# The turned g of the state tokens through V's two PSUM banks, and new places for the steps of the first two batches

## The chip, the cores and the metric

The kernel runs on one core of a Trainium2 chip. That core has five engines with an instruction queue each: TensorE (PE in the rows; PEld is its weight load), VectorE (DVE), ScalarE (ACT), GpSimd (POOL) and SyncE (SP), which issues nearly all the DMAs here. The metric is the device time of one execution in microseconds (us), lower being better. Three runs of the kernel before gave 486.24, 484.85 and 485.97 us, a median of 485.97 us.

## The reference, cut to what matters

Eight batches of 8 heads, 512 tokens and 32 state tokens go through attention in both directions. The result is 4608 rows of 512: eight times 512 tokens (the first part) and 32 state tokens. These rows go through a feed-forward layer with a piecewise activation, and then through a soft mixture of experts.

```python
def _attn_ref(x, state):                       # B, H, S, D = 8, 8, 512, 64; 32 state tokens
    a = softmax(x @ state^T / 8);   xread = a @ state
    a2 = softmax(state @ x^T / 8);  sread = a2 @ x
    return concatenate([xread, sread], axis=2)

def _moe_ref(x, w_in, w_out):                  # 4608 x 512, 512 x 2048, 2048 x 512
    h = x @ w_in
    g = np.where(h >= 1, h, np.where(h <= -1, 0.0, (h + 1) ** 2 / 4))
    return g @ w_out

def _moe2_ref(x, phi, w1, w2):                 # 8 experts of 4 slots
    logits = x @ phi
    slot_input = softmax(logits, axis=0)^T @ x
    slot_out[e] = relu(slot_input[e] @ w1[e]) @ w2[e]
    return softmax(logits, axis=1) @ slot_out
```

`w_in` and `w_out` come as 64-bit floats, and the kernel makes 32-bit floats of them on the chip.

## The kernel before

**Tiling.** The main loop goes over nine blocks `b`: the eight batches with 512 tokens each, and block 8 with the 256 state tokens of all batches. In each block `m` runs over 16 slices of 128 of the 2048 hidden columns. `attention(b)` makes the softmax of a batch, transposed; `vchunk(b, c)` multiplies the batch's state by a quarter `c` of `w_in`, so that `hstep(b, m)` gets a slice of h as V times the softmax, without the attention's output ever being made. In batch 0 h is two plain 32-bit products (line 529). From batch 1 on V and the softmax are each split into a high and a low half, and h is six products of halves (line 538): the high half is a ScalarE copy, the low half is V minus the high half, either by VectorE straight from PSUM (line 487) or by a second ScalarE copy `Vs` and a GpSimd subtraction (line 485). Lists in the table `CFG` (`lP0`, `lP1`, `lP`) name the pairs (c, G) that take the second way; G is one of the two PSUM banks of V. `Vs` shares its one buffer (`rot_q`) with `wsb` and `dR`.

**After h.** ScalarE makes c = relu(h/2 + 1/2); c is squared by GpSimd (letter E in `gv0`, `gv1`, line 568) or by ScalarE (letter S); VectorE makes g = min(max(h, 1), c) (line 592). The pool `psH` has three PSUM banks for h, so the fourth h after one waits until that one's g is made. VectorE turns g in blocks of 32x32 for later (`tstep`, line 612), `estep` multiplies a quarter of the g's by wp = w_out times phi, and `smblock` takes the running softmax over the tokens and accumulates g with its weights (`fall`, tiles FV and FX).

**The weights.** `conv_win(i)` for i = 0 to 7 and `conv_wo(i)` for i = 8 to 15 each turn a 1 MB stage of 64-bit words into 32-bit floats, by `words(i)`. For i in `dv` that is three VectorE instructions of 1024 columns (lines 154, 156, 158). For the others it is two byte moves into a rim (`LT`, `ast` or another tile), both by ScalarE or, for i in `pr`, the second by GpSimd (line 166), and two VectorE instructions (lines 170, 172). Two `conv_wo` make one of four `wps` products, whose ScalarE copy `wsb` is turned (line 197) and becomes a quarter of wp.

**Block 8.** The g of the state tokens are turned whole by TensorE: `tquarter(k)` (lines 601 to 609) turns four slices of 2x128 tokens, eight transposes of 128x128, into the tile gtp and copies them to `natS`. The tiles gtp come from `psH`, beside block 8's own h. `natS` is read by the products P in `smstate`, after which its buffers take weights of the experts. The experts' weights w1 and w2 (32 MB) are loaded by SP into whatever buffers come free, through the last third of the program.

**What sets the order.** For batches 2 to 7 TensorE's order is the order in which `steady` is written; everything else (batches 0 and 1, block 8, and the other engines throughout) is ordered by a scheduler when the program is built, from priorities in the order of the code. Lists of `CFG` say at which `m` a step is written: `cpos` the conversions, `at0` and `attA` the steps of attention 1 and 2, `V0` and `Vn` the V chunks, `E0` and `T0` the E quarters and the turned g's of batch 0, `a0n` how many steps of attention 0 come ahead of the first conversion. `warm` matmuls of 128x128 without use are issued behind the first scores.

Lines 116 and 122 are the helper `group` of matmuls side by side, line 127 the helper `act` of every ScalarE instruction.

Of the kernel before, what the change touches and what calls it, by code (L numbers as in the profile page):

```python
# [13 lines left out]
PSUM = bass.MemoryType.PSUM  # L14


CFG = {'no': 1, 'nl': 0, 'n0': (1, 12), 'nw': 512, 'nj': 'CABD', 'cw': (2, 2, 2, 4, 5, 6, 6, 7, 8, 8, 9, 11, 12, 13, 14, 15), 'pr': (0, 4), 'a0n': 6, 'w1p': (), 'r0': 0, 'sw': 1, 'whole': (4, 5, 6, 7), 'em': 8, 'lE': (0, 5, 8, 11), 'sV': (0, 4, 9, 12), 'sE': (7, 11, 15), 'sS': (1, 3, 5, 7), 'sN': 13, 'sM': (14, 14), 'gv7': 'EESESSSEESSSEEEE', 'cpos': (0, 1, 1, 3, 4, 4, 5, 7, 8, 10, 10, 12, 12, 15), 'at0': (5, 5, 5, 9, 9, 12, 13, 14, 14, 14), 'lP0': ((0, 0), (0, 1), (1, 0), (1, 1), (3, 0), (3, 1)), 'lP1': ((0, 1), (1, 0), (2, 0)), 'gv1': 'EEEEEEEEEESEEESE', 'f32': (0, 1, 2, 3), 'wsm': 14, 'xsP': 1, 'eng': ('PE',), 'wt8': (7, 8, 9, 10, 11, 12, 13, 14), 'wte': 'DA', 'wb': 12, 'gv6': (3, 5, 15), 'lP': ((0, 0), (0, 1), (1, 0), (2, 0), (3, 1)), 'attA': (3, 7, 9, 10, 11, 11, 11, 12), 'attB': (1, 11, 11, 12, 13), 'attN': (14, 15), 'dv': (3, 7, 8, 11), 'fl': -0.484375, 'hp': 2000, 'att7': (3, 5, 6, 7, 8, 10), 'og': 1, 'n3': 1, 'n3m': 10, 'wS': ('DP', 'PP', 'AD', 'PD', 'AP', 'DP', 'AP', 'AD', 'AD', 'DP', 'AD', 'AP', 'AP', 'AD', 'PD', 'AD'), 'xsm': 12, 'k0': 0, 'rg': 6, 'spg': 0, 'att0': 6, 'att': 7, 'V0': (2, 3, 4), 'Vn': (0, 2, 10), 'Vx': 12, 'wn': 'H', 'wsev': 'adad', 'conv': (4, 8, 9, 11, 12, 13, 19, 21, 24, 26, 28, 32, 36, 40, 44, 48, 52, 56, 60), 'todo': [1, 1, 1, 2, 0, 0, 0, 3, 0, 0, 2, 2, 1, 1, 0, 0], 'E0': ((0, 7), (0, 15), (0, 15), (1, 0)), 'T0': ((0, 8), (1, 0), (1, 0), (1, 0)), 'sm0': 6, 'E': 1, 'sm': 1, 'tqB': (5, 9, 13), 'GP': 0, 'pe': (3,), 'psH': 3, 'gtpX': (0, 7), 'tq0': (13, 15), 'keep': (2, 3, 4, 5), 'x2': (1, 0), 'natm': 1, 'warm': 18, 'bounce7': (0, 3), 'split': 1, 'wt': 0, 'so': '1011110001000010c1cc1', 'smm': (0, 0, 1, 2, 8, 10, 12), 'tqv': (), 'tqvm': 0, 'first': 'x', 'apath': 2, 'f32c': 1, 'place': 1, 'attm': (3, 6, 7, 8, 9, 12), 'subPm': True, 'loDm': False, 'bounce': (0, 1, 2, 3), 'bq': ('s', 's'), 'xq': 's', 'nat': ((1, 11), (2, 2), (2, 3), (2, 11), (3, 2), (3, 4), (3, 9), (4, 2), (4, 3), (4, 9), (5, 2), (5, 3), (5, 9), (6, 2), (6, 4), (6, 9)), 'subP': (1,), 'mulD': (), 'loD': (), 'qlag': 0, 'gv0': 'ESEEEEEESEEEEEEE', 'gv': 'EEEEEEESEEEESEEE', 'gvS': 'BEBBBBBBBBBSBEBB'}
# [1174 lines left out]
```

## Time and profile before

| what | us |
|---|---|
| median of three runs | 485.97 |
| the profiled execution | 484.75 |
| its span, first to last instruction | 482.9 |
| TensorE busy in the span | 437.1 |
| VectorE busy | 376.2 |
| ScalarE busy | 287.4 |
| GpSimd busy | 237.2 |

The profiled execution is 1.85 us longer than its span, and 1.22 us below the median of the runs. Busy shares are means over stages that have different limits: in the first 75 us VectorE is never idle for long, between 90 and 380 us TensorE hardly is, and from about 412 us on the weights' DMAs fill most of the time. Matmuls are pipelined, and their ends are modelled. "Idle before" in a row is the time for which the engine stood still ahead of the instruction, with what ended it.

### The profile page before, as it was taken

What the parts mean: (1) busy time and instruction counts of PE and PEld (TensorE: products, weight loads), DVE (VectorE), ACT (ScalarE), POOL (GpSimd) and SP (SyncE); (2) the same over time, 40 slices, a digit from 0 to 9 for tenths busy, and PEclk for the clock granted to TensorE, in tenths of its full rate; (3) what the DMA queues carried; (4) which work ended last, traced back from release to release, by engine and by line L of the source; (5) the groups of instructions that cost most, each with busy time, mean ns of one, the idle gap of its engine ahead of it and who ended that gap; (6) DMA issues with size and microseconds to landing.
All of it is one profiled execution on the core that took longest, in us unless ns stands there. A gap on an engine that the chain in (4) does not pass through costs nothing.

```text
span 482.9 us, 10684 instructions
## 1 busy us (share of the span) xinstructions
PE 437.1 (91%) x4320; PEld 247.1 (51%) x4320; DVE 376.2 (78%) x670; ACT 287.4 (60%) x528; POOL 237.2 (49%) x215
## 2 busy tenths in 40 slices
PE   5589799999999999999999999999999997999850
PEld 2333345555555565555655555665567775435330
DVE  2999998995999998999799899878888644440260
ACT  1887886547866975876787486475565363210350
POOL 4233349564865972984697297364065131120030
PEclk9799999999999999999999999999999998899995
DMA  8999632102213513433350355033054697799698
GB/s 302 420 419 420 280 136 88 72 19 88 88 41 139 216 44 132 162 146 115 107 209 11 132 200 194 1 129 135 14 207 174 230 399 287 299 419 417 256 354 305
DMA packets 19809, 94.21 MB, mean 195 GB/s; under 512 B 1840, under 2 KB 6320, under 8 KB 11184
## 3 DMA queue, kind: packets, MB, share of 16 engines
q1 hardware_dynamic: 19504, 93.00, 50.5%
q8 instruction: 34, 0.56, 0.5%
q0 software_dynamic: 256, 0.52, 0.5%
q14 instruction: 15, 0.12, 0.1%
HBM read 80.41 MB, written 13.11 MB: 194 GB/s over the span
## 4 chain that ended last, share of the span: by engine, by line
PE 38%; DVE 35%; DMA 8%; issue 6%; POOL 5%; ACT 4%; ACTq 0%; SPq 0%; POOLq 0%; DVEq 0%
PE h L538 13%; DVE gp L612 7%; DVE g L592 6%; DMA w<-in_w_dram 6%; PE h L546 5%; PE E L116 3%; PE FV L122 3%; POOL c L568 3%; PE FX L122 2%; DVE mx L294 2%; DVE m L313 2%; DVE att L297 2%; PE V L116 2%; DMA wb<-in_won_dram 2%; DVE z L335 2%
## 5 line engine op out<-in xcount | busy, mean ns | idle before, releaser
L538 PE MATMUL h<-a,v 128*128 128x512 f32 x672 | 175.9, 405 | 3.1 <-DVE g L592 2.3
L568 POOL TENSOR_TENSOR c<-c 128x512 f32<-128x512 f32 x107 | 115.9, 1086 | 104.0 <-ACT c L127 102.2
L538 PEld LDWEIGHTS h<-a,v 128*128 128x128 f32 x672 | 120.2, 188 | 78.1 <-issue 17.8
L127 ACT ACTIVATE c<-h,half 128x512 f32<-128x512 f32 x128 | 88.3, 691 | 69.2 <-PE h L538 55.6
L592 DVE SCALAR_TENSOR_TENSOR g<-h,c 128x512 f32<-128x512 f32 x112 | 74.7, 668 | 20.4 <-POOL c L568 17.8
L612 DVE STREAM_TRANSPOSE gp<-g 128x512 f32<-128x512 f32 x112 | 78.1, 700 | 1.1
L127 ACT ACTIVATE v<-V 128x512 fp32r<-128x512 f32 (+1 forms) x64 | 38.0, 601 | 7.4 <-DVE v L487 3.9
L485 POOL TENSOR_TENSOR v<-Vs,v 128x512 fp32r<-128x512 f32 x28 | 39.1, 1396 | 5.4 <-ACT Vs L127 5.3
L116 PE MATMUL V<-win,st_t 64*32 64x512 f32 x64 | 34.2, 615 | 3.7 <-ACT att L127 3.7
L122 PE MATMUL V<-win,st_t 64*32 64x512 f32 x448 | 36.5, 616 | 0.0
L529 PE MATMUL h<-spare,v 128*128 128x512 f32 x64 | 31.7, 627 | 4.5 <-DVE nb L295 2.4
L122 PE MATMUL FX<-gp,dR 32*32 32x512 f32 x512 | 35.6, 599 | 0.0
L122 PE MATMUL FV<-gp,dR 32*32 32x512 f32 x496 | 35.4, 597 | 0.0
L122 PE MATMUL E<-g,wp 128*32 128x512 f32 x168 | 29.5, 602 | 0.0
L116 PE MATMUL E<-g,wp 128*32 128x512 f32 x56 | 29.2, 602 | 0.1
L337 POOL TENSOR_TENSOR att<-att,z 128x512 f32<-128x512 f32 x16 | 18.6, 1165 | 18.1 <-DVE z L336 18.1
L546 PE MATMUL h<-XSh,v 128*128 128x256 f32 x128 | 25.0, 289 | 0.8 <-ACT v L127 0.4
L127 ACT ACTIVATE spare<-wb 128x512 uint8<-128x512 uint8 x32 | 24.0, 788 | 1.1 <-DMA wb<-in_won_dram 1.1
L1128 DVE COPY o<-oV 128x512 f32<-128x512 f32 x5 | 3.5, 691 | 25.8 <-PE oH L122 25.7
L529 PEld LDWEIGHTS h<-spare,v 128*128 128x128 f32 x64 | 11.6, 197 | 21.6 <-issue 10.2
L375 POOL TENSOR_TENSOR a<-att,a 128x512 fp32r<-128x512 f32 x14 | 19.7, 1421 | 5.7 <-ACT a L127 5.7
L546 PEld LDWEIGHTS h<-XSh,v 128*128 128x128 f32 x128 | 20.1, 188 | 3.4 <-DVE g L592 0.8
(248 smaller groups left out, 812.7 us busy)
## 6 DMA issues: line engine op xcount, KB each, us to landing
w<-in_w_dram SPq DMA_DIRECT2D x22, 1024.0 KB, 9.0
xn<-in_xn_dram SPq DMA_DIRECT2D x8, 1024.0 KB, 5.3
wb<-in_won_dram SPq DMA_DIRECT2D x8, 1024.0 KB, 5.5
xs<-in_xs_dram SPq DMA_DIRECT2D x7, 1024.0 KB, 4.8
gp<-in_w_dram SPq DMA_DIRECT2D x6, 1024.0 KB, 7.2
gp<-in_wout_dram SPq DMA_DIRECT2D x5, 1024.0 KB, 11.4
...
```

The source lines that it names most:

```text
L116: first = mm(**calls[0])
L122: e = mm(**c)
L127: return nc.scalar.activation(out=out, in_=in_, func=func, **kw)
L337: (nc.vector if b in CFG["mulD"] else nc.gpsimd).tensor_tensor(out=t3, in0=t3, in1=z1.unsqueeze(2).to_broadcast([128, 16, 32]), op=ALU.mult)
L375: (nc.vector if b in CFG["loD"] or b > 1 and CFG["loDm"] else nc.gpsimd).tensor_tensor(out=lo[:, G, :], in0=raw[G], in1=hi[:, G, :], op=AL ...
L485: nc.gpsimd.tensor_tensor(out=lo[:, G, :], in0=Vs, in1=hi[:, G, :], op=ALU.subtract)
L529: mm(out=h, lhsT=Vt[0, c][0][:, G, 128 * mm_:128 * mm_ + 128], rhs=araw[0][G], start=(G == 0), stop=(G == 1))
L538: mm(out=h, lhsT=v[:, G, f], rhs=a[:, G, :], start=(k == 0), stop=(k == 5))
L546: mm(out=h, lhsT=w[:, j, :], rhs=x[:, j, :], start=(k == 0), stop=(k == 11))
L568: nc.gpsimd.tensor_tensor(out=c, in0=c, in1=c, op=ALU.mult)
L592: gI[b, m] = nc.vector.scalar_tensor_tensor(out=g, in0=h, scalar=1.0, in1=c, op0=ALU.max, op1=ALU.min)
L612: nc.vector.transpose(out=gd_of(b, m), in_=gT[b, m])
```

## The change

The diff changes `tquarter`, and entries of the table `CFG`. In the file the table is one line; here its changed entries stand each on a line.

```diff
-'pr': (0, 4), 'a0n': 6,
+'pr': (0, 4, 6), 'a0n': 5,
-'cpos': (0, 1, 1, 3, 4, 4, 5, 7, 8, 10, 10, 12, 12, 15), 'at0': (5, 5, 5, 9, 9, 12, 13, 14, 14, 14),
+'cpos': (0, 0, 1, 2, 2, 3, 3, 7, 8, 10, 10, 10, 14, 14), 'at0': (4, 4, 7, 7, 9, 13, 14, 14, 14, 15),
-'lP0': ((0, 0), (0, 1), (1, 0), (1, 1), (3, 0), (3, 1)), 'lP1': ((0, 1), (1, 0), (2, 0)),
+'lP0': ((0, 1), (1, 0), (3, 0), (3, 1)), 'lP1': ((1, 0), (1, 1), (2, 0), (2, 1), (3, 0)),
-'gv1': 'EEEEEEEEEESEEESE', 'attA': (3, 7, 9, 10, 11, 11, 11, 12), 'dv': (3, 7, 8, 11),
+'gv1': 'EEEEEEEEEESEEEES', 'attA': (3, 3, 9, 9, 9, 10, 10, 12), 'dv': (3, 7, 8),
-'V0': (2, 3, 4), 'Vn': (0, 2, 10), 'E0': ((0, 7), (0, 15), (0, 15), (1, 0)),
+'V0': (1, 2, 4), 'Vn': (1, 2, 10), 'E0': ((0, 7), (0, 14), (0, 15), (1, 1)),
-'T0': ((0, 8), (1, 0), (1, 0), (1, 0)), 'warm': 18, 'gv0': 'ESEEEEEESEEEEEEE',
+'T0': ((0, 9), (0, 14), (1, 1), (1, 2)), 'warm': 26, 'gv0': 'SSEEEEEESEEEEEEE',
...
     def tquarter(k):
 
         natS[k] = rot_g.tile([128, 4, 512], F32, tag="g", name="natS") if k % 2 == 0 else natS[k - 1]
+        tp = psV.tile([128, 2, 512], F32, tag="V", name="gtp")
         for t in range(NS // 128):
-            tp = psH.tile([128, 512], F32, tag="H", name="gtp")
             for m4 in range(4):
-                nc.tensor.transpose(tp[:, 128 * m4:128 * m4 + 128],
+                nc.tensor.transpose(tp[:, t, 128 * m4:128 * m4 + 128],
                                     gT[B, 4 * k + m4][:, 128 * t:128 * t + 128], ident)
-            act(natS[k][:, 2 * (k % 2) + t], tp)
+        act(natS[k][:, 2 * (k % 2):2 * (k % 2) + 2], tp)
```

So the eleventh conversion gives up its three VectorE instructions for two byte moves and two; the sixth gives one of its byte moves to GpSimd, and the square of batch 0's first slice goes from GpSimd to ScalarE; in batch 1 the low half (0, 1) goes back to VectorE, and (1, 1), (2, 1) and (3, 0) go to GpSimd; the other entries move steps. The list `lP0` is read for chunks of batch 0 alone, and these return ahead of it.

VectorE from 51 us on, in the eleventh conversion (wD<-gp) and around it. In the kernel before:

```order
L154 TENSOR_SCALAR wD<-gp 128x1024
L295 TENSOR_SCALAR nb<-mx 128x1
L313 TENSOR_REDUCE m_405<-att 128x16
L592 SCALAR_TENSOR_TENSOR gp<-h,c 128x512
L156 SCALAR_TENSOR_TENSOR wD<-gp,wD 128x1024
L592 SCALAR_TENSOR_TENSOR gp<-h,c 128x512
L299 TENSOR_SCALAR rz<-sm 128x1
L294 TENSOR_REDUCE mx<-S 128x1
L297 STREAM_TRANSPOSE att<-S 128x512
L158 SCALAR_TENSOR_TENSOR wD<-gp,wD 128x1024
L334 TENSOR_REDUCE z_483<-att 128x16
L170 TENSOR_SCALAR wD<-wb_110 128x1024
```

In the kernel after:

```order
L170 TENSOR_SCALAR wD<-gp 128x1024
L295 TENSOR_SCALAR nb<-mx 128x1
L313 TENSOR_REDUCE m_448<-att 128x16
L592 SCALAR_TENSOR_TENSOR gp<-h,c 128x512
L172 SCALAR_TENSOR_TENSOR wD<-ast,wD 128x1024
L592 SCALAR_TENSOR_TENSOR gp<-h,c 128x512
L299 TENSOR_SCALAR rz<-sm 128x1
L294 TENSOR_REDUCE mx<-S 128x1
L297 STREAM_TRANSPOSE att<-S 128x512
L334 TENSOR_REDUCE z_491<-att 128x16
L300 RECIPROCAL rz<-rz 128x1
L170 TENSOR_SCALAR wD<-wb_110 128x1024
```

The three instructions of the conversion became two, and nothing else in the stretch moved but a short reciprocal.

ScalarE from 45 us on; LT<-gp is the tenth conversion's pair of byte moves, ast<-gp the eleventh's. In the kernel before:

```order
L127 ACTIVATE LT<-gp 128x1024 x2
L127 ACTIVATE c<-h,half 128x512 x2
L127 ACTIVATE c<-c 128x512
L127 ACTIVATE wsb<-wps 128x512
L127 ACTIVATE att,sm<-S,nb 128x512
```

In the kernel after:

```order
L127 ACTIVATE LT<-gp 128x1024 x2
L127 ACTIVATE c<-h,half 128x512
L127 ACTIVATE ast<-gp 128x1024 x2
L127 ACTIVATE c<-h,half 128x512
L127 ACTIVATE wsb<-wps 128x512
L127 ACTIVATE c<-c 128x512
L127 ACTIVATE att,sm<-S,nb 128x512
```

Two byte moves stand ahead of batch 0's ninth c, the copy wsb and the exponential of attention 1.

TensorE at the end of block 8, behind the last h (L546); E is the last quarter of the logits, LRs begins its softmax. In the kernel before:

```order
L546 MATMUL h<-XSh,v_564 128x256
L607 MATMUL gtp<-cst_t,s_gc 128x128 x6
L116 MATMUL E<-s_gc,wp 32x256
L122 MATMUL E<-s_gc,wp 32x256 x3
L607 MATMUL gtp<-cst_t,s_gc 128x128 x2
L672 MATMUL LRs<-eS,cst_t 128x256
```

In the kernel after:

```order
L546 MATMUL h<-XSh,v_568 128x256
L607 MATMUL gtp<-cst_t,s_gc 128x128 x2
L116 MATMUL E<-s_gc,wp 32x256
L122 MATMUL E<-s_gc,wp 32x256 x3
L607 MATMUL gtp<-cst_t,s_gc 128x128 x6
L672 MATMUL LRs<-eS,cst_t 128x256
```

On TensorE batch 0's last h (L529) also went ahead of the third of the four turns of `wsb` (L197), which it followed before. Four of the last quarter's transposes went from ahead of E to behind it; in the third quarter three of the eight behind E went ahead of it, among the h's.

## Rows read from the trace of the kernel before

**Rows 1.** Windows: length, busy us of PE, PEld, DVE, ACT, POOL; clock, DMA share, GB/s.
```profile
45.00:60.00 15.00, 12.94 (x63) 4.82 (x61) 15.00 (x23) 12.58 (x18) 6.17 (x5) 1.00 0.76 307
60.00:75.00 15.00, 13.88 (x139) 6.75 (x140) 15.00 (x27) 12.46 (x20) 8.18 (x6) 1.00 0.47 174
80.00:140.00 60.00, 58.49 (x534) 33.93 (x532) 53.46 (x105) 38.62 (x77) 39.74 (x38) 1.00 0.15 54
```

**Rows 2.** Timeline of VectorE around the eleventh conversion: start, length, instruction.
```profile
51.13 0.68 DVE L154 TENSOR_SCALAR wD<-gp 128x1024 uint32<-128x1024 uint32 x1
...
52.98 1.68 DVE L156 SCALAR_TENSOR_TENSOR wD<-gp,wD 128x1024 uint32<-128x1024 uint32 x1
...
56.48 1.18 DVE L158 SCALAR_TENSOR_TENSOR wD<-gp,wD 128x1024 uint32<-128x1024 uint32 x1
...
58.17 1.51 DVE L170 TENSOR_SCALAR wD<-wb 128x1024 uint32<-128x1024 uint32 x1
...
63.32 0.64 DVE L170 TENSOR_SCALAR wD<-wb 128x1024 uint32<-128x1024 uint32 x1
...
63.97 1.21 DVE L172 SCALAR_TENSOR_TENSOR wD<-LT,wD 128x1024 uint32<-128x1024 uint32 x1
```

**Rows 3.** Timeline of TensorE: start, length, instruction, idle time before and its releaser.
```profile
60.40 1.99 PE L529 MATMUL h<-spare,v 128*128 128x512 f32 x4 [2.38 <-DVE nb L295]
...
73.01 1.08 PE L197 MATMUL wps<-cst_t,wsb 128*128 128x32 f32 x8 [0.73 <-ACT wsb L127]
...
110.12 1.09 PE L324 MATMUL eTp<-cst_t,att 128*128 128x128 f32 x8
110.97 1.18 PE L538 MATMUL h<-a,v 128*128 128x512 f32 x4
```

**Rows 4.** Timeline of ScalarE: byte moves of the third, tenth and fourteenth conversion.
```profile
19.64 2.59 ACT L127 ACTIVATE LT<-ast 128x1024 uint8<-128x1024 uint8 x2
...
44.98 2.63 ACT L127 ACTIVATE LT<-gp 128x1024 uint8<-128x1024 uint8 x2
...
65.21 2.56 ACT L127 ACTIVATE LT<-gp 128x1024 uint8<-128x1024 uint8 x2 [0.73 <-DVE wD L172]
```

**Rows 5.** Timeline of GpSimd, and of VectorE beside its second instruction here.
```profile
23.90 1.72 POOL L166 COPY LT<-gp 128x1024 uint8<-128x1024 uint8 x1 [1.95 <-DVE win L172]
29.48 1.66 POOL L568 TENSOR_TENSOR c<-c 128x512 f32<-128x512 f32 x1 [3.87 <-ACT c L127]
...
30.16 2.06 DVE L172 SCALAR_TENSOR_TENSOR win<-win,win 128x1024 uint32<-128x1024 uint32 x1
```

**Rows 6.** Single lines, 60 to 140 us (minimum/median/maximum ns), and one group (mean ns).
```profile
L487 DVE TENSOR_TENSOR v<-V,v x7: 650/680/692, 70.4 to 139.7; 128x512 fp32r<-128x512 f32 x7
...
L485 POOL TENSOR_TENSOR v<-Vs,v x7: 1275/1285/1296, 77.5 to 137.9; 128x512 fp32r<-128x512 f32 x7
...
L127 ACT ACTIVATE Vs<-V 128x512 f32<-128x512 f32 x7 | 4.2, 597 | 0.3 <-POOL v L485 0.3
```

**Rows 7.** Timeline of ScalarE and TensorE at the end of block 8.
```profile
398.86 1.09 ACT L127 ACTIVATE natS<-gtp 128x512 f32<-128x512 f32 x2 [0.28 <-PE gtp L607]
...
399.60 0.36 PE L546 MATMUL h<-XSh,v 128*128 128x256 f32 x1 [0.34 <-ACT natS L127]
...
402.72 0.92 PE L607 MATMUL gtp<-cst_t,s_gc 128*128 128x128 f32 x6
404.40 0.40 PE L116 MATMUL E<-s_gc,wp 128*32 128x256 f32 x1 [0.76 <-DVE s_gc L596]
```

**Rows 8.** The chain that ended last, behind block 8: start, length, what.
```profile
411.04 0.87 PE P L122 x11
...
415.00 0.44 PE SI L122 x11
```

**Rows 9.** Windows of TensorE (busy, granted clock, DMA share, GB/s); SyncE's next issue.
```profile
408.00:412.00 4.00, 3.72 (x33) 0.50 0.34 141
...
411.94 8.03 SPq L814 DMA_DIRECT2D w<-in_w_dram  x7
```

More of the change, by code (lines that the diff above doesn't have):

```diff
@@ L14 @@
 PSUM = bass.MemoryType.PSUM
-CFG = {'no': 1, 'nl': 0, 'n0': (1, 12), 'nw': 512, 'nj': 'CABD', 'cw': (2, 2, 2, 4, 5, 6, 6, 7, 8, 8, 9, 11, 12, 13, 14, 15), 'pr': (0, 4), 'a0n': 6, 'w1p': (), 'r0': 0, 'sw': 1, 'whole': (4, 5, 6, 7), 'em': 8, 'lE': (0, 5, 8, 11), 'sV': (0, 4, 9, 12), 'sE': (7, 11, 15), 'sS': (1, 3, 5, 7), 'sN': 13, 'sM': (14, 14), 'gv7': 'EESESSSEESSSEEEE', 'cpos': (0, 1, 1, 3, 4, 4, 5, 7, 8, 10, 10, 12, 12, 15), 'at0': (5, 5, 5, 9, 9, 12, 13, 14, 14, 14), 'lP0': ((0, 0), (0, 1), (1, 0), (1, 1), (3, 0), (3, 1)), 'lP1': ((0, 1), (1, 0), (2, 0)), 'gv1': 'EEEEEEEEEESEEESE', 'f32': (0, 1, 2, 3), 'wsm': 14, 'xsP': 1, 'eng': ('PE',), 'wt8': (7, 8, 9, 10, 11, 12, 13, 14), 'wte': 'DA', 'wb': 12, 'gv6': (3, 5, 15), 'lP': ((0, 0), (0, 1), (1, 0), (2, 0), (3, 1)), 'attA': (3, 7, 9, 10, 11, 11, 11, 12), 'attB': (1, 11, 11, 12, 13), 'attN': (14, 15), 'dv': (3, 7, 8, 11), 'fl': -0.484375, 'hp': 2000, 'att7': (3, 5, 6, 7, 8, 10), 'og': 1, 'n3': 1, 'n3m': 10, 'wS': ('DP', 'PP', 'AD', 'PD', 'AP', 'DP', 'AP', 'AD', 'AD', 'DP', 'AD', 'AP', 'AP', 'AD', 'PD', 'AD'), 'xsm': 12, 'k0': 0, 'rg': 6, 'spg': 0, 'att0': 6, 'att': 7, 'V0': (2, 3, 4), 'Vn': (0, 2, 10), 'Vx': 12, 'wn': 'H', 'wsev': 'adad', 'conv': (4, 8, 9, 11, 12, 13, 19, 21, 24, 26, 28, 32, 36, 40, 44, 48, 52, 56, 60), 'todo': [1, 1, 1, 2, 0, 0, 0, 3, 0, 0, 2, 2, 1, 1, 0, 0], 'E0': ((0, 7), (0, 15), (0, 15), (1, 0)), 'T0': ((0, 8), (1, 0), (1, 0), (1, 0)), 'sm0': 6, 'E': 1, 'sm': 1, 'tqB': (5, 9, 13), 'GP': 0, 'pe': (3,), 'psH': 3, 'gtpX': (0, 7), 'tq0': (13, 15), 'keep': (2, 3, 4, 5), 'x2': (1, 0), 'natm': 1, 'warm': 18, 'bounce7': (0, 3), 'split': 1, 'wt': 0, 'so': '1011110001000010c1cc1', 'smm': (0, 0, 1, 2, 8, 10, 12), 'tqv': (), 'tqvm': 0, 'first': 'x', 'apath': 2, 'f32c': 1, 'place': 1, 'attm': (3, 6, 7, 8, 9, 12), 'subPm': True, 'loDm': False, 'bounce': (0, 1, 2, 3), 'bq': ('s', 's'), 'xq': 's', 'nat': ((1, 11), (2, 2), (2, 3), (2, 11), (3, 2), (3, 4), (3, 9), (4, 2), (4, 3), (4, 9), (5, 2), (5, 3), (5, 9), (6, 2), (6, 4), (6, 9)), 'subP': (1,), 'mulD': (), 'loD': (), 'qlag': 0, 'gv0': 'ESEEEEEESEEEEEEE', 'gv': 'EEEEEEESEEEESEEE', 'gvS': 'BEBBBBBBBBBSBEBB'}
@@ new lines @@
+CFG = {'no': 1, 'nl': 0, 'n0': (1, 12), 'nw': 512, 'nj': 'CABD', 'cw': (2, 2, 2, 4, 5, 6, 6, 7, 8, 8, 9, 11, 12, 13, 14, 15), 'pr': (0, 4, 6), 'a0n': 5, 'w1p': (), 'r0': 0, 'sw': 1, 'whole': (4, 5, 6, 7), 'em': 8, 'lE': (0, 5, 8, 11), 'sV': (0, 4, 9, 12), 'sE': (7, 11, 15), 'sS': (1, 3, 5, 7), 'sN': 13, 'sM': (14, 14), 'gv7': 'EESESSSEESSSEEEE', 'cpos': (0, 0, 1, 2, 2, 3, 3, 7, 8, 10, 10, 10, 14, 14), 'at0': (4, 4, 7, 7, 9, 13, 14, 14, 14, 15), 'lP0': ((0, 1), (1, 0), (3, 0), (3, 1)), 'lP1': ((1, 0), (1, 1), (2, 0), (2, 1), (3, 0)), 'gv1': 'EEEEEEEEEESEEEES', 'f32': (0, 1, 2, 3), 'wsm': 14, 'xsP': 1, 'eng': ('PE',), 'wt8': (7, 8, 9, 10, 11, 12, 13, 14), 'wte': 'DA', 'wb': 12, 'gv6': (3, 5, 15), 'lP': ((0, 0), (0, 1), (1, 0), (2, 0), (3, 1)), 'attA': (3, 3, 9, 9, 9, 10, 10, 12), 'attB': (1, 11, 11, 12, 13), 'attN': (14, 15), 'dv': (3, 7, 8), 'fl': -0.484375, 'hp': 2000, 'att7': (3, 5, 6, 7, 8, 10), 'og': 1, 'n3': 1, 'n3m': 10, 'wS': ('DP', 'PP', 'AD', 'PD', 'AP', 'DP', 'AP', 'AD', 'AD', 'DP', 'AD', 'AP', 'AP', 'AD', 'PD', 'AD'), 'xsm': 12, 'k0': 0, 'rg': 6, 'spg': 0, 'att0': 6, 'att': 7, 'V0': (1, 2, 4), 'Vn': (1, 2, 10), 'Vx': 12, 'wn': 'H', 'wsev': 'adad', 'conv': (4, 8, 9, 11, 12, 13, 19, 21, 24, 26, 28, 32, 36, 40, 44, 48, 52, 56, 60), 'todo': [1, 1, 1, 2, 0, 0, 0, 3, 0, 0, 2, 2, 1, 1, 0, 0], 'E0': ((0, 7), (0, 14), (0, 15), (1, 1)), 'T0': ((0, 9), (0, 14), (1, 1), (1, 2)), 'sm0': 6, 'E': 1, 'sm': 1, 'tqB': (5, 9, 13), 'GP': 0, 'pe': (3,), 'psH': 3, 'gtpX': (0, 7), 'tq0': (13, 15), 'keep': (2, 3, 4, 5), 'x2': (1, 0), 'natm': 1, 'warm': 26, 'bounce7': (0, 3), 'split': 1, 'wt': 0, 'so': '1011110001000010c1cc1', 'smm': (0, 0, 1, 2, 8, 10, 12), 'tqv': (), 'tqvm': 0, 'first': 'x', 'apath': 2, 'f32c': 1, 'place': 1, 'attm': (3, 6, 7, 8, 9, 12), 'subPm': True, 'loDm': False, 'bounce': (0, 1, 2, 3), 'bq': ('s', 's'), 'xq': 's', 'nat': ((1, 11), (2, 2), (2, 3), (2, 11), (3, 2), (3, 4), (3, 9), (4, 2), (4, 3), (4, 9), (5, 2), (5, 3), (5, 9), (6, 2), (6, 4), (6, 9)), 'subP': (1,), 'mulD': (), 'loD': (), 'qlag': 0, 'gv0': 'SSEEEEEESEEEEEEE', 'gv': 'EEEEEEESEEEESEEE', 'gvS': 'BEBBBBBBBBBSBEBB'}
```

## The prediction

> **What bounds the kernel now.** I read the busy times first, then the chain that ended last, then windows and timelines of the stretches that the diff touches. Three stretches have different limits. In the first 75 us VectorE is the limit: it is busy for 15.00 of 15 us in both windows [rows 1], while TensorE leaves 2.06 and 1.12 us unused, ScalarE 2.42 and 2.54. TensorE's largest stop there, 2.38 us ahead of the h at 60.40, ends when VectorE has made an older g and gets on [rows 3]. From about 80 us TensorE is the limit, so what the start saves arrives in full at the end: the frees of buffers, and the weights' loads that wait for them, only move ahead with it. From 412 us on the weights' DMAs set the end; their last flood starts when the products P have read natS (411.94) [rows 9]. A gain therefore has to come from VectorE before 75 us, from TensorE's stops in batch 1, or from the path through block 8 to P.
>
> **The eleventh conversion.** It gives up VectorE's 0.68 + 1.68 + 1.18 = 3.54 us and takes 0.64 + 1.21 = 1.85 us for the two-instruction form [rows 2]: 1.69 us less by lengths. Rows overlap by some 0.07 us each and one row falls away, so I count 1.6 us. VectorE's next 1024-wide instruction took 1.51 us at 58.17 where the same one took 0.64 at 63.32 [rows 2]; its place relative to GpSimd shifts, which is worth 0 to 0.87 us, and I take 0.3, since GpSimd's squares come just as often. TensorE thus resumes 1.9 us earlier than 60.40, inside the 2.38 us that it stood still [rows 3].
>
> The price lies on ScalarE: two byte moves, 2.63 us as a pair and 2.45 without the overlap [rows 4]. ScalarE had 2.42 us free between 45 and 60 us, so it becomes full there: 12.58 + 2.45 = 15.03 of 15 [rows 1]. Queued behind the pair are batch 0's ninth c, wsb and an exponential; TensorE's turn of wsb waits for them and starts some 0.4 us later, covered by its stop a few matmuls on. The fourteenth conversion's byte moves waited 0.73 us for VectorE [rows 4]; they now start when ScalarE gets to them, about 1.1 us earlier. TensorE waited 0.73 us for ScalarE's wsb at 73.01 [rows 3]; the last h of batch 0 now stands ahead of it, 1.99 us of work (the h at 60.40) [rows 3], and fills that gap. So the 1.9 us pass.
>
> **The sixth conversion and the first square.** One byte move goes to GpSimd (1.72 us) and one square of 1.66 us leaves it [rows 5], a few us apart. ScalarE gains half of 2.6 us and pays 0.6 for its square. In between stands VectorE, which does the same instructions in another order. I count nothing, with 0.3 us either way. Here a rule speaks against the change. An instruction of VectorE that ran beside GpSimd's square took 2.06 us [rows 5], where another of line 172 took 1.21 [rows 2]. The Trainium skill (SBUF — State Buffer, section "SBUF: two separate sides") says that VectorE and GpSimd share one pair of ports, which an instruction locks as a whole while the other engine's blocks. Counting the new byte move alone by that rule, VectorE would lose another 2.06 - 1.21 = 0.85 us and the sum below would be 0.65 us saved instead of 1.5: 485.3 us. Since the square leaves the same spot, I leave it at nothing.
>
> **The low halves of batch 1.** (0, 1) goes to VectorE; (1, 1), (2, 1), (3, 0) to ScalarE and GpSimd. VectorE does 0.68 us instead of 0.60 + 1.29 = 1.89 us on the other two engines [rows 6], a latency of 1.21 us more. VectorE's two subtractions fewer (1.3 us) are off the path, as TensorE is the limit there. (1, 1) and (2, 1) are made several slices before use: other work covers 1.21 us, and if that cover is gone each costs up to 1.21. (3, 0) has little cover. Behind V TensorE does eight transposes (0.85 us from start to start), then two h matmuls of the slice before and two of its own, some 0.25 to 0.3 each [rows 3], about 1.9 us. The low half is ready after the high copy, Vs and the subtraction, 0.60 + 0.60 + 1.29 = 2.5 us [rows 6]. TensorE stands still for some 0.6; the four h matmuls before took 1.18 us [rows 3], 0.2 more than undisturbed. Net 0.4 us lost, between 0 and 0.6.
>
> **The moved steps.** cpos, at0, attA, V0, Vn, E0, T0 and gv1 move VectorE's turns of g, TensorE's E's and attention steps among each other; the count of instructions is the same, SyncE's order as well. With TensorE full from 80 us on, only its stops matter: between 80 and 140 us it is idle for 60.00 - 58.49 = 1.51 us [rows 1]. Following the new order, one becomes longer: the accumulation FV needs V's banks, which attention 2's second exponential still reads, behind VectorE's second maximum. I count 0.2 us lost, with 0 and 0.8 as bounds. The eight more warm matmuls run while TensorE would stand still. The copies of V that follow wait in any case for ScalarE, whose byte moves last until 22.23 [rows 4]: nothing. lP0 changes nothing: it is not read.
>
> **The turned g of block 8.** Before, gtp took a bank of h's three, and TensorE waited 0.34 us for natS's copy [rows 7]; with the hand-over I count 0.4. V's banks are free in block 8 once the accumulation of batch 7 has been read, which the order allows for by putting the first quarter 21 matmuls later; behind a late read stands all of TensorE. The copy of 1024 columns instead of two of 512 (1.09 us [rows 7]) is not on the path, nor is natS's last one, as the softmax takes longer. Against it: six transposes instead of two stand between E and LRs. Six take 0.92 us [rows 7], and two of them ended just ahead of ScalarE's copy of E; the other four used to hide in the 0.76 us in which E waited for VectorE [rows 7]. At 0.13 each, less a slack that I put at 0.3, they cost 0.2. Net 0.2 us gained, between -0.2 and 0.5.
>
> **Sum.** 1.9 - 0.2 - 0.4 = 1.3 us at the start, 0.2 us at the end: 1.5 us. The profiled execution would fall from 484.75 to 483.25; it lies 1.22 us below the median of the runs, to which the same sum applies: 485.97 - 1.5 = 484.5 us.
>
> **Rival 1: ScalarE takes VectorE's place.** It is full from 45 to 60 us [rows 1], and if its order doesn't give, only the 1.1 us by which the fourteenth conversion starts earlier passes; less 0.6, plus 0.2, that is 0.7 us: 485.3. For it: the wait at 73.01 was already ScalarE's [rows 3]. Against it: that wait is now filled with an h.
>
> **Rival 2: the low halves hold TensorE, and it gets slower.** If GpSimd in batch 1 is late with (1, 1), (2, 1) and (3, 0), TensorE stops three times for 1.21 us: 3.6 us. Against 1.9 - 0.2 + 0.2 = 1.9 us that is 1.7 us lost: 487.7. It decides from the second of the three stops on. For it: GpSimd's work grows by 2.6 us, and Vs, wsb and dR share a buffer. Against it: (1, 1) and (2, 1) stand well ahead of their use.
>
> **Rival 3: the clock stays up at the end.** Between 408 and 412 us the granted clock is 0.50, that is 1.2 GHz, behind TensorE's pauses [rows 9]; a group of P took 0.87 us, one of SI at full clock 0.44 [rows 8]. If the transposes behind E keep it up, the 3.7 us that TensorE is busy there [rows 9] halve: 1.8 us more, 482.7 us. Against it: the waits for the softmax stay.
>
> **Rival 4: nothing moves,** as the savings are on engines off the path. Against it stands VectorE's full window [rows 1]. It gives 486.0.
>
> **How the numbers follow.** About 0.3% of this time (1.46 us) is what a measurement can tell from none. Forecast 0.50 (0.8 to 2.3 us saved: 0.28 faster, 0.22 same), rival 1 0.10 (same), rival 2 0.14 and other new stops 0.05 (slower), rival 3 0.10 (faster), rival 4 0.06 (same), and 0.05 that more of TensorE's stops go (faster). Faster 0.43, same 0.38, slower 0.19. The range from 482.3 to 486.6 us holds all but rival 2, the worse part of the other new stops and a little beyond rival 3: about 0.2 are left out.
>
> **What would show it.** Right: the h that started at 60.40 starts near 58.5, with less than 1 us of idle time; TensorE reaches batch 2 1 to 2 us earlier; no h waits for natS; P ends near 410.4 instead of 411.9. Wrong: ScalarE without a gap and TensorE waiting for wsb or c; a wait of h for GpSimd's v; VectorE's instructions near 30 us stretched; a clock that falls elsewhere.

## The result, and the profile after

The kernel after takes 481.54 us at the median (481.2 to 482.91, 4 runs), the kernel before 486.08 us in the same measurement: a ratio of 0.9917 with the 95% interval 0.9892 to 0.9943. Forecast were 484.5 us, within 482.3 to 486.6. It is faster, as was forecast, but by 4.5 us instead of 1.5, and lies below the range. A second measurement of both on another chip (after_b below) gave 482.42 beside 484.78 us, 0.9951 (0.9926 to 0.9975). Times of one and the same kernel here spread over 2 to 6 us, and a profile shows one execution; so the parts are read from instants in the traces, and the times are set beside them.

The windows of the profiled execution (span 479.4 us) that answer to [rows 1, 9]; columns as there:

```profile
45.00:60.00 15.00, 13.76 (x66) 5.33 (x65) 14.85 (x24) 15.00 (x21) 5.51 (x5) 1.00 0.88 354
33.00:39.00 6.00, 5.26 (x23) 1.88 (x23) 6.00 (x8) 2.93 (x7) 2.03 (x2) 0.72 1.02 425
80.00:140.00 60.00, 58.41 (x540) 34.22 (x533) 52.28 (x105) 40.33 (x82) 43.15 (x40) 1.00 0.16 54
408.00:412.00 4.00, 3.74 (x64) 1.98 (x60) 0.92 (x2) 0.77 (x2) 0.52 (x1) 1.00 0.68 250
```

ScalarE is now the full engine from 45 to 60 us (15.00 of 15). The granted clock falls in a new place, 33 to 39 us, and no longer at 408 us. TensorE's timeline (start, length, instruction, idle time before with its releaser), which answers to [rows 3, 7]:

```profile
33.74 3.66 PE L529 MATMUL h<-spare,v 128*128 128x512 f32 x4 [2.04 <-DVE gp L592]
...
53.89 1.08 PE L197 MATMUL wps<-cst_t,wsb 128*128 128x32 f32 x8 [1.24 <-ACT wsb L127]
...
58.13 3.70 PE L529 MATMUL h<-spare,v 128*128 128x512 f32 x8
62.91 0.66 PE L324 MATMUL eTp<-cst_t,att 128*128 128x128 f32 x4 [1.08 <-ACT att L127]
...
100.29 0.61 PE L116 MATMUL FV<-gp,dR 32*32 32x512 f32 x1 [0.78 <-ACT att L127]
...
393.55 0.38 PE L607 MATMUL gtp<-cst_t,s_gc 128*128 128x128 f32 x2
...
394.01 0.27 PE L607 MATMUL gtp<-cst_t,s_gc 128*128 128x128 f32 x1
...
403.01 0.40 PE L116 MATMUL E<-s_gc,wp 128*32 128x256 f32 x1 [1.46 <-DVE s_gc L596]
...
403.58 0.87 PE L607 MATMUL gtp<-cst_t,s_gc 128*128 128x128 f32 x6
404.29 0.60 PE L672 MATMUL LRs<-eS,cst_t 128*128 128x256 f32 x2
406.20 0.31 PE L682 MATMUL dNp<-cst_t,eS 32*128 32x32 f32 x2 [1.31 <-ACT eS L127]
```

The h that waited 2.38 us at 60.40 starts without a stop, joined to the one before it: it is the second four of the eight at 58.13, and starts at 59.95. In its place stand two stops that ScalarE ends, 1.24 and 1.08 us. Four h at 33.74 took 3.66 us at the low clock. No h of block 8 waits for natS any more; the longest wait of one for ScalarE is 0.09 us, at 394.38. The chain that ended last, and SyncE's next issue, answer to [rows 8, 9]:

```profile
407.44 0.45 PE P L122 x11
...
410.37 0.45 PE SI L122 x11
```

```profile
408.78 11.20 SPq L814 DMA_DIRECT2D w<-in_w_dram  x10
```

A group of P takes 0.45 us instead of 0.87, and the weights' loads go on at 408.78 instead of 411.94.

**All executions side by side.** Starts in us from the timelines of TensorE, one profiled execution a line: the first FV; the product with acc (line 756), which closes the batches; from it to the last E of block 8; from the first P to the first SI, the product that makes the experts' inputs; the first product of the experts (L1053); the first SR, which sums the experts' outputs SO behind their last weights (L1095); and the span.

| kernel | FV | acc | acc to E | P to SI | L1053 | SR | span |
|---|---|---|---|---|---|---|---|
| before | 100.77 | 386.60 | 17.80 | 4.89 | 418.85 | 450.23 | 482.9 |
| before_b | 100.96 | 386.55 | 17.76 | 4.88 | 418.95 | 450.17 | 482.6 |
| cfg: table alone | 99.62 | 385.41 | 17.79 | 4.52 | 416.82 | 450.39 | 483.6 |
| cfg_b | 99.65 | 385.53 | 17.78 | 2.93 | 415.35 | 447.23 | 479.5 |
| tq: turn alone | 100.77 | 386.18 | 16.63 | 2.93 | 414.89 | 448.14 | 480.7 |
| tq_b | 100.86 | 386.37 | 16.62 | 2.93 | 415.07 | 447.11 | 479.5 |
| after | 100.29 | 386.38 | 16.63 | 2.93 | 415.09 | 447.11 | 479.4 |
| after_b | 99.58 | 385.40 | 16.62 | 2.93 | 414.10 | 448.94 | 481.6 |

From before to after_b the 4.75 us at L1053 are 1.20 from the table (acc), 1.18 from the turn (acc to E), 1.96 from the clock (P to SI), and 0.41 between these places. Of the 4.75 us 1.3 are left at the end of the span in that execution; in the first one 3.5 of 3.76.

### The profile page after: what moved, and what is told of

Read it like the earlier page. It is cut to its first block, busy times and chain, and to the rows that moved or that the text cites. A ratio compares the mean times of both kernels' runs of the same rounds, so it can differ in the third digit from the quotient of the medians.

```text
span 479.4 us, 10721 instructions
## 1 busy us (share of the span) xinstructions
PE 435.4 (91%) x4336; PEld 247.3 (52%) x4336; DVE 374.4 (78%) x667; ACT 289.2 (60%) x528; POOL 239.5 (50%) x217
## 4 chain that ended last, share of the span: by engine, by line
PE 49%; DVE 28%; DMA 6%; ACT 5%; issue 5%; POOL 4%; ACTq 0%; SPq 0%; POOLq 0%; DVEq 0%
PE h L538 17%; DVE gp L612 6%; DVE g L592 5%; PE h L546 5%; PE E L116 3%; DMA w<-in_w_dram 3%; PE FV L122 3%; PE V L116 3%; PE h L1053 3%; POOL c L568 2%; PE h L529 2%; PE FX L122 2%; DVE mx L294 2%; DMA wb<-in_won_dram 2%; DVE z L335 1%
## 5 line engine op out<-in xcount | busy, mean ns | idle before, releaser
L568 POOL TENSOR_TENSOR c<-c 128x512 f32<-128x512 f32 x106 | 114.6, 1084 | 97.1 <-ACT c L127 95.3
L592 DVE SCALAR_TENSOR_TENSOR g<-h,c 128x512 f32<-128x512 f32 x112 | 74.7, 668 | 20.1 <-POOL c L568 17.0
L485 POOL TENSOR_TENSOR v<-Vs,v 128x512 fp32r<-128x512 f32 x30 | 41.7, 1389 | 9.5 <-ACT Vs L127 9.5
L529 PE MATMUL h<-spare,v 128*128 128x512 f32 x64 | 32.5, 644 | 2.2 <-DVE gp L592 2.0
L337 POOL TENSOR_TENSOR att<-att,z 128x512 f32<-128x512 f32 x16 | 17.2, 1076 | 18.1 <-DVE z L336 18.1
L546 PE MATMUL h<-XSh,v 128*128 128x256 f32 x128 | 25.2, 289 | 0.1
L529 PEld LDWEIGHTS h<-spare,v 128*128 128x128 f32 x64 | 11.9, 202 | 20.2 <-issue 13.5
L546 PEld LDWEIGHTS h<-XSh,v 128*128 128x128 f32 x128 | 20.2, 189 | 2.6 <-DVE g L592 0.8
```

Source lines behind the costliest of these rows:

```text
L337: (nc.vector if b in CFG["mulD"] else nc.gpsimd).tensor_tensor(out=t3, in0=t3, in1=z1.unsqueeze(2).to_broadcast([128, 16, 32]), op=ALU.mult)
L485: nc.gpsimd.tensor_tensor(out=lo[:, G, :], in0=Vs, in1=hi[:, G, :], op=ALU.subtract)
L529: mm(out=h, lhsT=Vt[0, c][0][:, G, 128 * mm_:128 * mm_ + 128], rhs=araw[0][G], start=(G == 0), stop=(G == 1))
L546: mm(out=h, lhsT=w[:, j, :], rhs=x[:, j, :], start=(k == 0), stop=(k == 11))
L568: nc.gpsimd.tensor_tensor(out=c, in0=c, in1=c, op=ALU.mult)
L592: gI[b, m] = nc.vector.scalar_tensor_tensor(out=g, in0=h, scalar=1.0, in1=c, op0=ALU.max, op1=ALU.min)
```

## Experiments

In the diffs `fill(n)` stands for n matmuls of 128x128 on constants, whose result nobody reads, put in a stop of TensorE; one takes 0.24 us. They shift the line numbers in their kernels (L1106 is SO there). Ratios are to the kernel before on the same chip, with the 95% interval.

**The two halves.** One kernel has the new `tquarter` with the old table, the other the reverse.

> The kernel before with the turned g alone changed (V's banks, one copy a quarter), the table as it was. Theory: the whole gain is here. Block 8's h lose their two stops (0.43 and 0.34 us) and shorter transposes, so that the last E starts about 1.2 us earlier than 404.40; behind it the granted clock stays 1.00, so that from the first P to the first SI it takes 2.9 us instead of 4.89. Sum 3.2 us: 482.9 us. Rival, the prediction's sizes: 0.2 us, 485.9 us, clock 0.50 from 407 us on as before.

> The kernel after with the old turned g (h's banks, two copies a quarter), so the table's changes alone. Theory: they bring what the two traces show at 148.8 and 343.7 us, 0.1 to 0.2 us: 485.9 us, and at the end the clock falls to 0.50 behind the last E as in the kernel before, with 4.9 us from the first P to the first SI. Rival, the prediction's sizes: 1.3 us less, 484.8 us. Second rival, that it only depends on the instant at which block 8 comes whether the clock falls: 2 us less with the clock at 1.00, 484.0 us.

Measured: 483.24 us, 0.9968 (0.9952 to 0.9984), and 482.99 us, 0.9966 (0.9947 to 0.9985), beside 484.88. Each is worth about 1.6 to 1.9 us at the median. That is against the theory, which gave the table 0.1 to 0.2 us: the first trace of the kernel after had misled me, since the clock had fallen at 33.7 us in it. The turn shows 1.2 us to the last E and the clock at 1.00 behind it, as its theory had it, but gives 1.6 us in all, not 3.2.

**The kernel after once more, and with the old warm-up.**

```diff
-'warm': 26
+'warm': 18
```

> The kernel after once more, on the chip of the next three. Theory: two gains of about 1.2 us each that every execution has (table: the product with acc starts at 385.4 instead of 386.6 where the clock stays up; turn: the last E 1.2 us earlier against that product), and on top falls of the clock that sit elsewhere in each execution (seen so far at 33.7, 60, 407 and 443 to 465 us, at 0.5 to 2 us and more). Then it lies 2.4 to 3.5 us under the kernel before, and its runs spread over some 2 us. Rival, that the turn keeps the clock up by itself: over 3.5 us under it in every run, with a spread under 1 us.

> The kernel after with 18 warm matmuls instead of 26; nothing else in any engine's order moves. Theory: the granted clock falls and rises again as in the kernel before (0.50 from 18 to 24.6 us), the four h that start at 33.74 run at full clock and take 1.99 us instead of 3.66; TensorE then waits longer for VectorE and ScalarE, which are full from 30 to 64 us, so of the 1.67 us 0 to 0.5 pass: 481.0 to 481.5 us. Rival, that the low clock at 34 us ate the table's gain: 1.2 us less than the kernel after, 480.3 us.

Measured: 482.42 us (480.32 to 485.73, 12 runs), 0.9951; and 481.54 us, 0.9936 (0.9915 to 0.9957). In after_b the same order of instructions ran with the four h at full clock, behind a stop that was no shorter; with 18 warm matmuls the clock fell there all the same. Timelines of TensorE, after_b and then the old warm-up:

```profile
33.60 1.98 PE L529 MATMUL h<-spare,v 128*128 128x512 f32 x4 [2.42 <-DVE gp L592]
```

```profile
33.75 3.51 PE L529 MATMUL h<-spare,v 128*128 128x512 f32 x4 [1.88 <-DVE gp L592]
```

So the warm matmuls don't decide it. What the fall costs is 0.7 us at the first FV (100.3 instead of 99.6) and 0.8 to 1.0 us at acc (386.2 to 386.4 instead of 385.4). So the rival of warm18 had nearly the right price, though the clock fell in its profile too. In after_b the runs spread over 5.4 us; that excludes its rival, that the turn alone keeps the clock up, with a spread under 1 us.

**The clock at P.** Three kernels with the old turn and fillers near LRs: hold_end has ten behind LRs, fill_before four, and fill_E two ahead of it, behind the last E. Beside them stand second executions of before, of the table alone and of the turn alone. The edits of fill_before and of fill_E, cut:

```diff
         act(al, nmo, ACTF.Exp, scale=-1.0, bias=nm)
+        fill(4)
...
     estep(B, 3)
+    fill(2)
```

> The kernel before with ten matmuls of 128x128 without use behind LRs, in the stop of 1.31 us in which TensorE waits for the softmax of block 8; they take some 1.2 us. Theory: the clock stays at 1.00 there, from the first P to the first SI it takes 2.9 us instead of 4.89, and the program gets 1.9 us shorter, 484.2 us. Rival, that the clock's price is hidden behind the loads of the weights: within 0.3 us of the kernel before, 486.0 us, whatever the clock does.

> The kernel before with the same matmuls in the same three stops. Theory: the clock stays at 1.00 behind LRs, 2.9 us from the first P to the first SI; the median drops by 1.2 to 2.0 us against the kernel before, and the filled kernel after is still 2.4 us faster than this one, since those gains have nothing to do with the clock. Rival, that the turn's gain is mainly the clock's: the filled kernel after is only 1.0 to 1.4 us faster than this one.

> The kernel before with two matmuls of 128x128 without use between the last E and LRs, about 0.48 us of work at the place where the new turn has four transposes more. Theory: that work keeps the clock up, 2.93 us from the first P to the first SI instead of 4.89, and the median lies 1.0 to 1.7 us under the kernel before, as with the fillers in the three late stops. Rival: what counts is how long TensorE worked without a stop ahead of it (the h's stops of 0.43 and 0.34 us), and the clock falls as before: 4.5 to 4.9 us, the time within 0.3 us.

> The kernel before once more, one look. Theory: as in the first profile the clock falls at P (4.5 to 4.9 us from the first P to the first SI), since the stops ahead of it come in every execution at the same distances. Rival, that the instant decides: in about half of such looks it stays up, 2.93 us.

> The table's changes alone, once more, one look. Theory: the old turn lets the clock fall at P, 4.5 to 4.9 us from the first P to the first SI. Rival: the instant decides, 2.93 us in about half of the looks.

> The turn alone, once more, one look. Theory: the new turn keeps the clock up at P, 2.93 us from the first P to the first SI. Rival: the instant decides, 4.5 us or more in about half of the looks.

Measured: hold_end 484.1 us, 0.998 (0.9967 to 0.9994); its ten fillers lasted 2.39 us, not 1.2, and put P off by 0.7 us. fill_before, which has fillers ahead of two groups of SO too, 483.14 us, 0.9968 (0.9952 to 0.9985); the kernel after with the same fillers (fill_after, below) is 1.5 us faster on that chip, nearer the rival's 1.0 to 1.4 than the theory's 2.4. fill_E 483.16 us, 0.998 (0.9961 to 0.9999), so 1.3 us by the medians, at the edge of what can be told. The second executions of before, cfg and tq took 484.51, 481.32 and 481.53 us. P to SI took 2.93 us in each of the three with fillers. Windows of before_b and of fill_E (length, busy us of PE, PEld, DVE, ACT, POOL; clock, DMA share, GB/s):

```profile
406.00:412.00 6.00, 4.38 (x36) 1.90 (x36) 1.99 (x8) 1.35 (x5) 0.00 (x0) 0.61 0.60 219
```

```profile
406.00:412.00 6.00, 4.12 (x56) 2.07 (x58) 2.40 (x8) 2.67 (x8) 1.03 (x2) 1.00 0.81 265
```

With the old turn the clock fell in three of four executions without fillers (4.89, 4.88, 4.52; not in cfg_b), with the new turn in none of seven (tq, tq_b, after, after_b, warm18, dv11, pr6b). With some half a microsecond of work between E and LRs, without anything else of the turn, it did not fall in the one profile of fill_E, nor in one of the four without that work. The instant has its part too: cfg and cfg_b have one order of instructions, and in one the clock fell. And tq2c, below, has the new bank and four transposes behind LRs, and it fell there from 405.4 us on. So the turn seems to make the fall at P rarer; how much rarer, and by which of its pauses, some ten traces can't say.

**Bank or copy.** tq2c is the kernel before with the new bank, but with two copies a quarter as of old. Its edit against the turn alone:

```diff
-        act(natS[k][:, 2 * (k % 2):2 * (k % 2) + 2], tp)
+            act(natS[k][:, 2 * (k % 2) + t], tp[:, t])
```

> The kernel before with the turned g in V's two banks, but with two copies of 512 columns for each quarter as before, so that the change of bank stands alone. Theory: the gain is the bank's, since h no longer waits for natS and the transposes can go where h stands still; from the product with acc to the last E it takes 16.6 us as with one copy (17.80 before). Rival: the single copy is what counts, as two of them stand ahead of v and s_gc on ScalarE: 17.3 us or more.

Measured: 484.03 us, 0.9979 (0.9965 to 0.9993). Acc to E takes 16.3 us (387.32 to 403.65), no longer than with one copy: the gain is the bank's. But here four transposes stand behind LRs, the clock fell (P to SI 4.79 us), and the time is 0.8 us above the turn alone. In this profile, with the old table, the clock also fell at the start, from 33.3 to 36.8 us:

```profile
33.48 3.59 PE L529 MATMUL h<-spare,v 128*128 128x512 f32 x4 [2.21 <-DVE gp L592]
```

The first FV then starts at 101.51 instead of 100.77, as much later as with the new table. So the fall that the kernel after shows there is not the new table's own.

**The eleventh conversion.**

```diff
-'dv': (3, 7, 8)
+'dv': (3, 7, 8, 11)
```

> The kernel after with the eleventh conversion's three instructions back on VectorE; ScalarE loses its two byte moves. Theory of the prediction: VectorE's 1.9 us pass to the end, so this is 1.2 to 1.9 us slower than the kernel after. Rival: ScalarE, 15.00 of 15 us busy between 45 and 60 us, has taken VectorE's place, and TensorE's waits of 1.24 us for wsb and 1.08 us for the softmax's exponential go when it gets the byte moves off: the same time within 0.4 us.

Measured: 482.76 us, 0.9952 (0.9931 to 0.9974), beside 482.42 for after_b. Times can't tell the two apart, and 0.3 us is the rival's number. The traces can. TensorE and the engines' window from 45 to 60 us in dv11, then TensorE in after_b; its last row is the second four of the eight h at 57.32, from a view that begins with them:

```profile
61.07 1.98 PE L529 MATMUL h<-spare,v 128*128 128x512 f32 x4 [2.31 <-DVE nb L295]
```

```profile
45.00:60.00 15.00, 13.04 (x63) 4.84 (x61) 15.00 (x22) 13.35 (x19) 6.51 (x5) 1.00 0.75 294
```

```profile
57.32 3.74 PE L529 MATMUL h<-spare,v 128*128 128x512 f32 x8
62.09 0.66 PE L324 MATMUL eTp<-cst_t,att 128*128 128x128 f32 x4 [1.03 <-ACT att L127]
```

```profile
59.14 1.92 PE L529 MATMUL h<-spare,v 128*128 128x512 f32 x4
```

In dv11 ScalarE has 1.65 us free again, and the stop of 2.31 us at the old place is back; the h behind it starts at 61.07 instead of 59.14. FV starts at 100.67 instead of 99.58, acc at 386.57 instead of 385.40: the eleventh conversion is worth 1.1 to 1.2 us on TensorE's path. That is all of the table's gain there, since dv11 lies at the kernel before (386.60 at acc).

**The sixth conversion, and fillers at the start.** pr6b takes back the sixth conversion's byte move and the first square; late_start is the kernel late, below, with five more fillers behind the second V chunk of batch 0. Both edits let the scheduler order batches 0 and 1 anew. That of pr6b, cut:

```diff
-'pr': (0, 4, 6) ... 'gv0': 'SSEE...'
+'pr': (0, 4) ... 'gv0': 'ESEE...'
```

> The kernel after with the sixth conversion's second byte move back on ScalarE and the first square back on GpSimd. The prediction counted nothing for the two, 0.3 us either way. Theory: VectorE's first instruction of 1.72 us beside GpSimd's byte move at 31.37 takes 0.7 again, but ScalarE has 1.35 us more ahead of the c's there, so the h at 33.7 starts within 0.5 us of that, and the time is that of the kernel after within 0.4 us. Rival, the port: VectorE gains 1 us, the first FV starts near 98.9 instead of 99.6 us, and the time is 0.7 us less.

> The same with five more fillers behind the second V of batch 0, in the stop of 2.04 to 2.42 us ahead of the h at 33.7; the scheduler also moves some steps of the first two batches. Theory: the four h run at full clock in every execution, and the product with acc starts near 385.4 us instead of 386.4 wherever the clock would have fallen: 0 to 1 us faster than without, on the median 0.4. Rival: the steps moved cost as much as the clock gives, and the first FV starts later than 100.3 us.

Measured: 488.14 us, 1.0086 (1.0054 to 1.0117), and 489.01 us, 1.0083 (1.0067 to 1.0099). Neither theory holds; late_start's rival does, that the moved steps cost more than the clock gives. Both lose some 6 us against the kernel after, and all of it by the second FV, the one of batch 1: it starts at 145.75 and 146.28 us instead of 139.67 in after_b. In late_start it is lost by the first FV already (106.47 instead of 99.58), in pr6b 3.6 us of it (103.21). The largest stop of pr6b between the two, on TensorE and on VectorE ahead of it:

```profile
125.36 4.57 PE L538 MATMUL h<-a,v 128*128 128x512 f32 x12 [3.02 <-DVE g L592]
```

```profile
121.44 0.69 DVE L294 TENSOR_REDUCE mx<-S 128x1 f32<-128x512 f32 x1 [3.14 <-PE S L122]
122.05 0.70 DVE L297 STREAM_TRANSPOSE att<-S 128x512 f32<-128x512 f32 x1
...
123.94 0.64 DVE L313 TENSOR_REDUCE m<-att 128x16 f32<-128x512 f32 x1
...
124.62 0.68 DVE L592 SCALAR_TENSOR_TENSOR g<-h,c 128x512 f32<-128x512 f32 x1
```

VectorE waits 3.14 us for the next scores S and does eight steps of their softmax before the g for which TensorE waits. In late_start the four h at 33.67 do run at full clock (1.98 us), and it is of no use. So the sixth conversion couldn't be tried alone.

**The end.** Fillers ahead of the last groups of SO in the kernel after: SO are the products with the experts' last weights. Both kernels have four fillers behind LRs; ahead of groups of SO fill_after has two and four, late three, four and four (the diff).

```diff
             place, w = where["w2", 8 * dh + e]
+            fill({12: 3, 13: 4, 14: 4}.get(group, 0))
```

> The kernel after with matmuls of 128x128 without use in three late stops of TensorE: four behind LRs (about 1 us of 1.31), two and four ahead of the thirteenth and fourteenth group of SO, which wait for the last weights. Theory: falls of the clock behind 404 us go, so that the median drops by 0.3 to 0.8 us against the kernel after and the spread of the runs gets below 1.5 us. Rival, that stops of this length cost nothing in the kernel after, since its profile shows 1.00 there: the same time within 0.2 us.

> The kernel after with matmuls of 128x128 without use in TensorE's late stops: four behind LRs, and three, four and four ahead of the thirteenth, fourteenth and fifteenth group of SO (stops of 1.05, 1.42 and 1.44 us ahead of these groups; a filler takes 0.24 us at full clock). Theory: the clock no longer falls between 445 and 450 us, as it did in the profiles of the turn alone, of the kernel after's second one and of the one with the eleventh conversion undone (0.66 to 0.68 there, about 1.2 us each); the median is 0.6 to 1.2 us under 482.4. Rival: what the last loads of weights bring sets that stretch, and nothing changes within 0.3 us.

Measured: 481.68 us (480.95 to 485.41), 0.9948 (0.9926 to 0.997), and 482.27 us, 0.9947 (0.9929 to 0.9965), both within noise of after_b: fill_after's median is 0.7 us lower on the same chip, but its runs still spread over 4.5 us. TensorE in after_b, then in late:

```profile
446.22 2.79 PE L1088 MATMUL SO<-w,hTD 128*32 128x256 f32 x24 [1.44 <-DMA w<-in_w_dram]
448.94 0.78 PE L1095 MATMUL SR<-tail,cst_t 128*128 128x256 f32 x2
```

```profile
445.62 1.16 PE L120 MATMUL fillw<-cst_t 128*128 128x128 f32 x8
446.71 0.64 PE L1106 MATMUL SO<-w,hTD 128*32 128x256 f32 x8
447.28 0.70 PE L1114 MATMUL SR<-tail,cst_t 128*128 128x256 f32 x2
```

Late had the clock at 1.00 there and the shortest span of all, 479.1 us; its median doesn't follow. In fill_after the clock was up as well and SR, which stands behind the last weights, started at 450.06, 3 us later than in the kernel after. So late's rival holds for the median. Between two executions of one order SR varies by 0.1 us (before) to 3.2 us (cfg, where 1.6 of them are the clock at P), by 1.8 us in the kernel after. No kernel here is clearly faster than the kernel after.

## Why the prediction was right and wrong

**The eleventh conversion: right, oversized.** The forecast was 1.9 us on TensorE's path, 1.3 us for the table after its losses. Against dv11, whose edit is the conversion alone, the h behind the old stop starts 1.93 us earlier and without a stop: VectorE's saving has the size that was forecast. Against the kernel before it is less: 59.14 in after_b and 59.95 in the kernel after, where the clock had fallen, instead of 60.40; 58.5 was forecast. At the first FV and at acc dv11 gives 1.1 to 1.2 us for the conversion, and the rest of the table nothing. What fell short was "so the 1.9 us pass": ScalarE, full as foreseen, stops TensorE in after_b at 53.08 (1.24 us) and at 62.09 (1.03 us). That is rival 1's mechanism, at part of its price.

**The sixth conversion: right at nothing.** The rows show the exchange. GpSimd, and VectorE beside it, in the kernel after:

```profile
30.26 2.27 POOL L166 COPY LT<-wb 128x1024 uint8<-128x1024 uint8 x1 [4.68 <-DVE win L172]
```

```profile
30.12 1.22 DVE L172 SCALAR_TENSOR_TENSOR win<-win,win 128x1024 uint32<-128x1024 uint32 x1
31.37 1.72 DVE L170 TENSOR_SCALAR win<-wb 128x1024 uint32<-128x1024 uint32 x1
```

Line 172 takes 1.22 us where it took 2.06 [rows 5], and line 170 takes 1.72 where 0.68 is usual: 0.84 us back, 1.04 lost, and the h behind it starts at 33.74 in the kernel after and at 33.60 in after_b, where it was 33.60 before. The Trainium skill's lock on the shared ports (SBUF — State Buffer, section "SBUF: two separate sides") agrees with these rows: VectorE's instruction of 1.72 us ends at 33.09, 0.56 us behind GpSimd's. On GpSimd's side they show less: its copy took 0.55 us longer than the one in [rows 5], while line 172 ran beside it for 1.08 us.

**The low halves of batch 1: wrong, to the good.** I took 0.4 us for (3, 0), and rival 2 had 3.6 us. No h of batch 1 waits for v in the kernel after or in after_b; TensorE's busy time between 80 and 140 us (58.41) is that of before (58.49, [rows 1]). The one wait for a low half is a product of V's, for VectorE's subtraction (line 487): 0.39 us at 76.97, in after_b 0.52 us at 76.27. I had not listed it.

**The moved steps: right.** FV waits for attention 2's exponential, 0.78 us at 100.29, where before an h had waited 0.47 (at 99.18): 0.3 us more, and I counted 0.2 lost.

**The clock at 34 us: not priced.** The prediction has "a clock that falls elsewhere" as a sign of being wrong, and no term for it. Where it falls, TensorE loses 1.7 us on four h and 0.8 to 1.0 at acc. It fell in three of the seven profiles that keep the new table's order there (after, warm18, fill_after), and not in after_b, cfg, cfg_b, late; and it fell in tq2c, with the old table. My "nothing" for the warm matmuls isn't contradicted: the fall came with 26 and with 18 of them, and moves with the execution.

**The turned g: the step that failed.** The forecast was 0.4 us less 0.2, "between -0.2 and 0.5"; acc to E is 1.13 to 1.18 us shorter in every trace of the new turn with one copy. I counted only the stop for natS. Up to the last h of block 8 TensorE gains 1.33 us over the same 84 h and 16 transposes (14.67 us from acc instead of 16.00). Of these 0.34 us are natS's stop. Another 0.34 come from a second stop in the same stretch, in the kernel before:

```profile
394.80 0.38 PE L546 MATMUL h<-XSh,v 128*128 128x256 f32 x1 [0.43 <-ACT v L127]
```

The transposes, freed from h's banks, now stand in it (393.55 and 394.01 above), and 0.09 us of it are left. The largest part, 0.65 us, is no stop at all: the same matmuls take less time where the transposes stand among h's in groups of one to five than eight in a row. Why, no run here shows, and as the ends of matmuls are modelled, the split between stops and work is rough. 0.15 us are lost again ahead of E, whose stop grows from 0.76 to 1.46 us, since the four transposes that stood in it went behind E. Their price there was right: E to LRs 1.28 us instead of 1.14.

**The clock at P: the wrong chance.** Rival 3 named it: transposes behind E keep the clock up, 1.8 us. It measured 1.96, with one chance in ten given to it, and outside the sum; my ground against it, that the waits for the softmax stay, was true (1.31 us in both) and no ground. At L1053 after_b is 4.75 us ahead where the sum had 1.5: 1.0 us of the difference is the turn's term and 2.0 the clock's.

**"Arrives in full at the end": wrong.** Up to L1053 the gains add up; behind it only part of them is left, and TensorE waits for the last weights. DMA windows of before and after (the last two columns are share and GB/s):

```profile
410.00:415.00 5.00, 4.99 (x52) 2.14 (x48) 0.96 (x2) 0.77 (x2) 0.52 (x1) 0.61 0.40 129
```

```profile
410.00:415.00 5.00, 4.61 (x72) 2.85 (x64) 0.85 (x2) 1.38 (x5) 0.41 (x1) 1.00 0.93 382
```

In these 5 us the loads stood still for the like of 3.0 us (a share of 0.40) and now for 0.35. That this hole's closing is the gain that the end sees is argued, and not tested by itself: in the five profiles with a share under 0.7 there (before, before_b, cfg, hold_end, tq2c) SR starts at 449.7 to 450.4 us, in the others, pr6b and late_start left out, at 447.1 to 450.1. Then the DMAs run full until 446 us, and TensorE stops for them three times in after_b (1.05, 1.42, 1.44 us). What the 4.5 us of the first measurement owe to lucky executions can't be told; the second one says 2.4, less than the 3.7 us saved that the range allowed.

Three of the prediction's signs of being wrong came true: ScalarE without a gap and a wait for wsb (1.24 us), a stretched instruction of VectorE near 30 us (1.72 us), and a clock that fell elsewhere. The kernel is faster all the same; they cost part of the table's gain, and what was not foreseen lies in block 8.
